# One attention kernel of two parts: three phases against eight interleaved chunks with a hand-kept order

## The chip, the cores and the metric

The kernel runs on one core of one Trainium2 chip. The metric is the device time of one execution in microseconds, from many executions of which the fast ones of a kernel agree within about 1.5%. "The profile" is one execution recorded by the hardware profiler; "the trace" is its list of instructions. The clock of TensorE is recorded as a share of its full speed. "Busy" is the recorded time of an engine's instructions.

## The reference

Two independent attentions over 2048 tokens with 32 heads of 20 columns (width 640); the outputs stand side by side.

```python
# A: four segments of 512 tokens; causal softmax inside a segment, plus a memory of earlier segments
for s in range(4):
    p = softmax(qs @ ks.T * scale + causal_mask);  a_dot = p @ vs
    pq = phi(qs);  a_mem = (pq @ M) / (pq @ z + 1e-6)      # phi(t) = t+1 if t>0 else exp(t)
    outs.append(g * a_mem + (1 - g) * a_dot)
    M = M + phi(ks).T @ vs;  z = z + phi(ks).sum()
A = concat(outs) @ wo
# B: causal attention in a sliding window of 256 tokens
B = (softmax(mask_window(q @ k.T * scale)) @ v) @ wo
```

## The kernel before

Heads are handled four at a time (a "group", eight groups), each head in its own 32 rows. The *scores* k·q of a head contract over 32 rows, so they use a 32-row tile of the array; the *values* p·v produce 32 output rows, so they use a 32-column tile. All projections, output projections and transposes use the whole array ("dense" below). The exponentials run on ScalarE, masks on GpSimd and VectorE, evacuations of PSUM on VectorE. (PSUM is the memory that TensorE writes to; an evacuation copies a result out of it.) The tile that a matmul uses, whole array, 32 rows, 32 columns or both, is called its tiling mode below, and a step from one to another a mode change.

The program has three phases: all projections of B and the k, v projections of A; then attention B, with the q projection of A interleaved as long as it lasts; then attention A with the output projections. This is B's inner loop:

```python
for kt in range(T):                                        # 16 key tiles of 128
    for hp in range(2):                                    # scores: two heads per PSUM tile
        for i in range(2):
            nc.tensor.matmul(pss[hp][:, i, 0:N], lhsT=kg[rows, ...], rhs=qg[rows, ...],
                             tile_position=(HD * q4, 0))   # a 32-row tile
    ...                                                    # exp on ScalarE, masks
    if kt % 2 == 1:
        for hp in range(2):
            for i in range(2):                             # values: head by head
                for n_, (_, k2, oc0, ncol, rc0) in enumerate(entries):
                    nc.tensor.matmul(O[orows, oc0:oc0 + ncol], lhsT=vg[:, k2, q4, 0:HD],
                                     rhs=pts[(hp, k2)][:, i, rc0:rc0 + ncol],
                                     tile_position=(0, HD * q4))   # a 32-column tile
        ...                                                # evacuate, transpose, normalise
    next(aux_gen, None)                                    # one piece of A's q projection
```

A's values (line 462) have the same order, hp, i, then key tile.

The softmax here doesn't subtract the row's maximum and nothing guards it: scores larger than these inputs give would overflow.

## Time and profile before

| | before |
|---|---|
| time, median of the first five runs | 808.9 us |
| TensorE / ScalarE / VectorE / GpSimd busy | 710 / 374 / 422 / 245 us |
| mean granted TensorE clock | 0.708 |

From the profile page of the kernel before: the first line's "busy us (share) xinstructions" of TensorE (PE), then the busy tenths of TensorE and ScalarE (ACT) in 40 slices of the span, and the granted clock in tenths.

```profile
...
PE 710.1 (88%) x4736; PEld 307.5 (38%) x4768; DVE 421.9 (52%) x1013; ACT 374.2 (46%) x498; POOL 244.9 (30%) x498
...
PE   2779969999999899999999888889988899889987
...
ACT  0000000046567876676665776246660666336650
...
PEclk9999989999999855555555555685558655585559
...
```

ScalarE does next to nothing (1.5 us) in the first fifth. The clock is near full in the first third and about half in most of the rest.

From the view by stretches of the kernel before; the columns are the stretch, its length, then busy us (and count) of TensorE, its weight loads, VectorE, ScalarE and GpSimd, and then the clock, the DMA share and GB/s.

```profile
...
120.00:160.00 40.00, 38.60 (x207) 18.76 (x210) 24.31 (x35) 0.00 (x0) 0.00 (x0) 1.00 0.58 183
240.00:280.00 40.00, 36.25 (x301) 17.15 (x300) 24.64 (x83) 30.91 (x46) 17.82 (x38) 0.98 0.55 165
278.00:430.00 152.00, 145.55 (x891) 55.57 (x889) 68.75 (x248) 104.76 (x143) 56.55 (x126) 0.50 0.11 31
...
```

For 152 us TensorE is busy 96% of the time and yet has half the clock. The q projection of A, the only projection in this phase, had run out at 252 us; of dense work only 70 transposes of 128 columns are left in the stretch, 13.8 us of TensorE. The Trainium skill ("TensorE: Matmul & The Clock Gate", Part 1) says that the clock is gated to half unless the array has been busy; that "busy" evidently isn't the busy time of the profile.

From the page, the chain that ended last, by engine. It is followed back from the last instruction, at each step to what ended that one's wait, its releaser:

```profile
...
PE 59%; DVE 10%; ACT 9%; POOL 8%; issue 6%; SPq 4%; DMA 2%; ACTq 0%; DVEq 0%; POOLq 0%
...
```

From the view of groups by form: line, engine, operation and shapes, count, then busy us and mean ns of one, and then idle time before and its releasers.

```profile
...
L305 ACT ACTIVATE pt<-psS 128x768 bf16<-128x768 f32 x224 | 171.7, 810 | 237.9 <-PE psS L298 197.8 <-issue 25.3 <-DVE oc L226 10.6
L437 ACT ACTIVATE pt<-ps 128x1024 bf16<-128x1024 f32 x128 | 126.9, 1023 | 85.2 <-PE ps L429 80.2 <-PE ps L462 4.5
...
```

### The profile page before, as it was taken

What the parts mean: (1) busy time and instruction counts of PE and PEld (TensorE: products, weight loads), DVE (VectorE), ACT (ScalarE), POOL (GpSimd) and SP (SyncE); (2) the same over time, 40 slices, a digit from 0 to 9 for tenths busy, and PEclk for the clock granted to TensorE, in tenths of its full rate; (3) what the DMA queues carried; (4) which work ended last, traced back from release to release, by engine and by line L of the source; (5) the groups of instructions that cost most, each with busy time, mean ns of one, the idle gap of its engine ahead of it and who ended that gap; (6) DMA issues with size and microseconds to landing.
All of it is one profiled execution on the core that took longest, in us unless ns stands there. A gap on an engine that the chain in (4) does not pass through costs nothing.

```text
span 807.3 us, 12210 instructions
## 1 busy us (share of the span) xinstructions
PE 710.1 (88%) x4736; PEld 307.5 (38%) x4768; DVE 421.9 (52%) x1013; ACT 374.2 (46%) x498; POOL 244.9 (30%) x498
## 2 busy tenths in 40 slices
PE   2779969999999899999999888889988899889987
PEld 1334524444444433333333333443335333443334
DVE  5356666566666544444444342555556455454435
ACT  0000000046567876676665776246660666336650
POOL 9000060024334433343333334113430333213430
PEclk9999989999999855555555555685558655585559
DMA  9923315641213604101000000420005000010001
GB/s 217 269 100 131 131 32 154 202 135 53 86 53 121 207 1 138 32 1 34 1 1 1 1 2 1 144 78 1 1 6 202 17 1 2 1 66 1 0 1 66
DMA packets 54028, 54.26 MB, mean 67 GB/s; under 512 B 22802, under 2 KB 46482, under 8 KB 53970
## 3 DMA queue, kind: packets, MB, share of 16 engines
q1 hardware_dynamic: 53970, 53.49, 21.6%
q8 instruction: 37, 0.61, 0.3%
q14 instruction: 21, 0.17, 0.1%
HBM read 24.38 MB, written 23.07 MB: 59 GB/s over the span
## 4 chain that ended last, share of the span: by engine, by line
PE 59%; DVE 10%; ACT 9%; POOL 8%; issue 6%; SPq 4%; DMA 2%; ACTq 0%; DVEq 0%; POOLq 0%
PE psO L341 11%; PE ps L462 10%; POOL pt L443 7%; PE psS L298 6%; ACT pt L437 6%; PE ps L262 5%; DVE oc L226 5%; PE pps L181 4%; PE ps L429 4%; PE pps L147 4%; PE pps L197 3%; PE ppa L181 3%; ACT pt L305 3%; SPq L528 2%; PE ps L228 2%
## 5 line engine op out<-in xcount | busy, mean ns | idle before, releaser
L305 ACT ACTIVATE pt<-psS 128x768 bf16<-128x768 f32 (+2 forms) x256 | 185.5, 770 | 247.3 <-PE psS L298 201.8
L437 ACT ACTIVATE pt<-ps 128x1024 bf16<-128x1024 f32 (+1 forms) x192 | 162.0, 882 | 97.3 <-PE ps L429 88.4
L443 POOL TENSOR_SCALAR_AFFINE_SELECT pt<-pt 128x256 bf16<-128x256 bf16 x256 | 107.0, 438 | 238.2 <-ACT pt L437 235.3
L313 POOL TENSOR_SCALAR_AFFINE_SELECT pt<-pt 128x256 bf16<-128x256 bf16 x224 | 104.2, 465 | 219.8 <-ACT pt L305 219.8
L462 PE MATMUL ps<-pt,v_s 128*32 128x128 bf16 (+3 forms) x512 | 117.9, 455 | 11.3 <-POOL pt L443 7.4
L341 PE MATMUL psO<-pt,vaug_B 128*32 128x256 bf16 (+1 forms) x960 | 125.5, 315 | 0.7 <-DVE pt L307 0.4
L307 DVE TENSOR_TENSOR pt<-pt,cmask 128x256 bf16<-128x256 bf16 x256 | 80.0, 313 | 52.0 <-ACT pt L305 50.5
L298 PE MATMUL psS<-qg,kg 32*128 32x384 bf16 (+2 forms) x512 | 100.2, 412 | 6.7 <-ACT pt L305 5.3
L429 PE MATMUL ps<-q_s,k_s 32*128 32x128 bf16 (+3 forms) x512 | 93.3, 433 | 7.5 <-ACT pt L437 6.0
L341 PEld LDWEIGHTS <-vaug_B 128*32 128x32 bf16 x960 | 59.8, 110 | 68.8 <-issue 57.2
L226 DVE CAST oc<-ps 128x512 bf16<-128x512 f32 x56 | 38.6, 689 | 79.4 <-PE ps L462 77.3
L462 PEld LDWEIGHTS <-v_s 128*32 128x32 bf16 x512 | 39.3, 119 | 75.4 <-issue 73.2
L226 DVE CAST oc<-psO 128x256 bf16<-128x256 f32 x64 | 27.1, 424 | 60.2 <-PE psO L341 60.1
L147 PE MATMUL pps<-xT_B,wallB 128*128 128x512 bf16 x196 | 47.4, 404 | 8.4 <-DMA wallB<-in_B_wqkv_dram 4.0
L228 PEld LDWEIGHTS <-oc 128*128 128x128 bf16 x352 | 27.7, 119 | 61.5 <-DVE oc L226 60.8
L298 PEld LDWEIGHTS <-kg 32*128 32x128 bf16 x512 | 25.1, 96 | 57.9 <-issue 50.1
L429 PEld LDWEIGHTS <-k_s 32*128 32x128 bf16 x512 | 20.4, 100 | 69.5 <-issue 67.6
L181 PE MATMUL ppa<-xT_A,wq_padA 128*128 128x512 bf16 x149 | 42.6, 380 | 4.3 <-DVE stp L184 2.4
L228 PE MATMUL ps<-ident,oc 128*128 128x128 bf16 x224 | 33.3, 302 | 14.5 <-DVE oc L226 14.5
L181 PE MATMUL pps<-xT_A,wk_padA 128*128 128x512 bf16 x156 | 36.6, 392 | 7.4 <-DVE wk_padA L133 6.9
L270 DVE CAST otile<-ps 128x640 bf16<-128x640 f32 x32 | 26.4, 825 | 23.0 <-PE ps L266 22.3
L147 PEld LDWEIGHTS <-wallB 128*128 128x128 bf16 x200 | 20.5, 103 | 34.6 <-issue 9.9
(95 smaller groups left out, 672.9 us busy)
## 6 DMA issues: line engine op xcount, KB each, us to landing
out_dram<-otile SPq DMA_DIRECT2D x32, 160.0 KB
vdA<-vstA SPq DMA_DIRECT2D x8, 512.0 KB
kdA<-stp SPq DMA_DIRECT2D x4, 1024.0 KB
qdA<-stp SPq DMA_DIRECT2D x4, 1024.0 KB
k_s<-kdA SPq DMA_DIRECT2D x4, 1024.0 KB
v_s<-vdA SPq DMA_DIRECT2D x4, 1024.0 KB
q_s<-qdA SPq DMA_DIRECT2D x4, 1024.0 KB
kcdB<-kcB SPq DMA_DIRECT2D x1, 2560.0 KB
```

The source lines that it names most:

```text
L147: nc.tensor.matmul(ps[:, 0:512], lhsT=w_ap[:, kt, m * P:(m + 1) * P], rhs=xT[:, kt, cs], start=(kt == 0), stop=(kt == KT - 1))
L181: nc.tensor.matmul(ps[:, 0:512], lhsT=wpad[:, kt, g * P:(g + 1) * P], rhs=xT[:, kt, cs], start=(kt == 0), stop=(kt == KT - 1))
L226: nc.vector.tensor_copy(out=oc[:, 0:ncols], in_=num_ps[:, 0:ncols])
L298: nc.tensor.matmul(pss[hp][:, i, 0:N], lhsT=kg[rows, kt * P:(kt + 1) * P], rhs=qg[rows, kt * P:kt * P + N], start=True, stop=True, tile_po ...
L305: nc.scalar.activation(out=pt[:, :, 0:N], in_=pss[hp][:, :, 0:N], func=ACT.Exp, scale=scale)
L307: nc.vector.tensor_tensor(out=pt[:, :, 0:P], in0=pt[:, :, 0:P], in1=self.cmask[:].unsqueeze(1).to_broadcast([P, 2, P]), op=ALU.mult)
L313: nc.gpsimd.affine_select(out=blk, in_=blk, pattern=[[0, 2], [-1, P]], compare_op=ALU.is_ge, fill=0.0, base=-1, channel_multiplier=1)
L341: nc.tensor.matmul(O[orows, oc0:oc0 + ncol], lhsT=vg[:, k2, q4, 0:HD], rhs=pts[(hp, k2)][:, i, rc0:rc0 + ncol], start=(n_ == 0), stop=(n_ ...
L429: nc.tensor.matmul(pss[hp][:, i, coloff[kt]:coloff[kt] + n], lhsT=k_s[rows, g, q0:q0 + P], rhs=q_s[rows, g, q0:q0 + n], start=True, stop=True,
L437: nc.scalar.activation(out=pt[:, :, 0:used], in_=pss[hp][:, :, 0:used], func=ACT.Exp, scale=scale)
L443: nc.gpsimd.affine_select(out=blk, in_=blk, pattern=[[0, 2], [1, P]], compare_op=ALU.is_ge, fill=0.0, base=0, channel_multiplier=-1)
L462: nc.tensor.matmul(NUM[orows, P * kt:P * kt + n], lhsT=v_s[:, kt, h, 0:HD], rhs=pt[:, i, co:co + n], start=(cnt == 1), stop=(cnt == nmm), ...
```

## The change

The intent: keep TensorE and ScalarE busy at the same time from start to end. The kernel is nearly rewritten; this is its core.

```diff
-  phase 1: all projections; phase 2: attention B (+ A's q projection); phase 3: attention A
+  chunks = [("A", 0), ("B", 0), ("A", 1), ("B", 1), ("A", 2), ("B", 2), ("A", 3), ("B", 3)]
+  # every chunk: 512 queries, 8 groups x 3 score banks x 2 head pairs = 48 "slots" (384 in all)
+  with self.tc.manual_schedule():            # instructions stay in the order they are written
+      for t, (n, kind, c, banks, g, b, pair) in enumerate(slots):
+          if t == start[n]: seed(n + 1)      # projections of the next chunk become filler
+          fl.force(t)                        # filler whose deadline is now
+          pt = self.scores(banks, b, pair, g, k, q, koff)      # + one exp of up to 1024 columns
+          self.masks(...)
+          # finished group: values 3 slots later, transposes 5, normalisation 6 slots later
+          fl.run(t, extra, kind == "A" and c > 0 and t % 2 == 1)   # filler, as credit allows
 ...
+  def av(...):                               # values: key tile by key tile, over the four heads
+      for n_, (_, kt, q0, nq, b, c0) in enumerate(ent):
+          for j in range(4):
+              nc.tensor.matmul(O[HD * j:HD * j + HD, ...], ..., tile_position=(0, HD * j))
 ...
+  def final_job(self, o_tok, b, wo, out_rows):    # output projection as filler, 32 jobs
+      transposes; yield 5 * mm_ns(128)
+      nc.vector.tensor_copy(out=oT[:], in_=t[:, 0:self.KT * P])
+      yield 600.0
+      for hf in range(2): 5 matmuls of 320 columns each; copy to ot
+      nc.sync.dma_start(out=out_rows, in_=ot[:])
 ...
-  A's q and k projected with padded weights: 8 blocks of 128 rows for each 512 columns
+  projected compactly (5 blocks), stored to DRAM, and spread to 32 rows a head by DMA
```

`fl` is a queue of generators. It gives each slot as much filler as spreads what is left evenly, and with the last argument true it gives none.

## The prediction

> **What bounds the kernel now (808.9 us).** Three phases. The view by stretches shows projections in 0-160 us, with ScalarE busy only 1.5 us; then sliding-window attention B until about 510 us; then segments A. TensorE bounds it: 710 us busy (88%), 59% of the chain that ended last; ScalarE 374, VectorE 422, GpSimd 245. Two things make TensorE slow. (1) The granted clock is about 1.00 until 278 us, then 0.50 except in bursts at the output projections (mean 0.71). From 280 to 440 us TensorE is busy 38.3 of every 40 us and still gets 0.50; what had ended was the dense 128-row q projection of A, interleaved until 252 us. The Trainium skill ("TensorE: Matmul & The Clock Gate", Part 1) says activity releases the throttle; here narrow 32-row/32-column work alone did not suffice. (2) In the timeline, the attention-times-values matmuls (lines 341, 462) run head by head: in A the next tile of a head starts about 390, 310, 100 ns after the last at half clock, so four heads take about 3.4 us.
>
> **What the change does.**
> - Eight chunks (A, B alternating), with projections, output projections and memory updates as filler between score tiles: the serial 160 us goes, and dense work (half of TensorE's time) spreads over the span, so I expect a clock near 1.0.
> - Attention times values goes key tile by key tile over four heads: tiled neighbours start 3 to 13 ns apart in the trace, so 512+384+256+128 columns should take about 0.53 us at full clock.
> - Exps of B are 192 of up to 1024 columns, not 256 of 768; A's q/k projections lose their padding (8 blocks to 5), except in chunk 0.
> - Added: spreading of heads through DRAM by strided DMAs, and many alternations of tiling mode. A change of mode costs 95-100 ns at full clock in the trace (dense to score 310 against 215; score to value 260 against 160). The Trainium skill ("TensorEngine Tiling (Array Packing)", Key Properties) calls it a drain; the trace agrees.
>
> **Sums (estimates from durations in the trace).** TensorE at full clock: scores 73, values 37, memory and updates 10, q/k projections 93, v 43, output 52, transposes 24, so about 330; plus about 700 mode changes in the built order at 95 ns, 67: about 396 us. ScalarE: 0.94 us for 1024 columns back to back, 0.73 for 768: 325 plus 33 phi exps 20, about 345. VectorE about 335 (fewer masks and casts), GpSimd 285. So TensorE still bounds, ScalarE close behind. Start: the first projection began at 27 us; now one 512-row chunk and one weight suffice, about 11 us. 11 + 396 + 5 cold start + 4 at the end = 416 if TensorE never waits. For waits on exps, evacuations and chunk boundaries I add 5 to 12%: **448 us, range 415 to 500**. Faster by over 2%: 0.97; within 2%: 0.02; slower: 0.01. Practically all of the gain lies on the critical path, as TensorE is the path.
>
> **What would show it.** Mean clock above 0.9; TensorE over 90% busy, ScalarE 75-85%; first exp before 20 us; the four value matmuls of one key tile about 13 ns apart; mode changes of about 95 ns; VectorE about 335 us.
>
> **What would make it wrong.** The clock falls to 0.5 in chunks with little filler (the last B chunk, or odd slots in A, where filler is held). Column-tiled matmuls interleaved over heads may not overlap. VectorE evacuations with four shared PSUM buffers, VectorE and GpSimd slowing each other, or DMA spreading at chunk boundaries could stall the in-order TensorE queue above 12%. If TensorE and ScalarE overlap better: about 420.

## More of the kernel before

An output projection transposes a token tile on TensorE, copies it with VectorE and multiplies it at once. The order of instructions on each engine is the framework's scheduler's; it may move them as the dependencies allow.

From the timeline of TensorE in the kernel before, in a later segment of A: start, duration until the last of the merged matmuls ended, line, tile names, count.

```profile
...
564.14 0.61 PE L462 MATMUL ps<-pt,v_s 128*32 128x512 bf16 x1
564.68 0.39 PE L429 MATMUL ps<-q_s,k_s 32*128 32x256 bf16 x2
565.01 0.88 PE L462 MATMUL ps<-pt,v_s 128*32 128x384 bf16 x2
565.82 0.61 PE L429 MATMUL ps<-q_s,k_s 32*128 32x256 bf16 x4
566.75 1.25 PE L462 MATMUL ps<-pt,v_s 128*32 128x256 bf16 x8 [0.32 <-POOL pt L443]
567.94 0.60 PE L429 MATMUL ps<-q_s,k_s 32*128 32x512 bf16 x1
568.48 1.25 PE L462 MATMUL ps<-pt,v_s 128*32 128x256 bf16 x5
569.66 0.60 PE L429 MATMUL ps<-q_s,k_s 32*128 32x512 bf16 x2
...
```

Line 462 is the values of one group, 16 matmuls, and line 429 is scores of the next group. The scheduler has cut the 16 value matmuls into pieces of 1, 2, 8 and 5, with scores between. From the first value matmul to the last piece's end is 5.6 us, at a clock of 0.50.

## The result, and the profile after

The changed kernel takes 485.9 us (median of nine; one of them, 496.5, counts as slow), the kernel before 809.7 us beside it. The ratio is 0.600 (0.5987 to 0.6011); here and below a ratio is the mean time of a kernel's fast runs over that of the other's of the same rounds, so it is not quite the ratio of the medians. The time lies within the predicted range, 38 us above the central value.

| | before | after | predicted |
|---|---|---|---|
| span in the profile | 807.3 | 484.2 | |
| TensorE busy | 710 | 421 (87%) | over 90% |
| ScalarE busy | 374 | 356 (74%) | 345 (75 to 85%) |
| VectorE / GpSimd busy | 422 / 245 | 323 / 263 | 335 / 285 |
| mean clock | 0.708 | 0.974 | over 0.9 |
| first exp of a score | 169.0 | 15.7 | before 20 |

The page of the changed kernel, same lines:

```profile
...
PE 421.3 (87%) x4770; PEld 195.6 (40%) x4806; DVE 322.8 (67%) x690; ACT 356.3 (74%) x419; POOL 263.4 (54%) x551
...
PE   2999998898978998979896999898988799899965
...
ACT  1346678879677777878986777697888677799930
...
PEclk9999999899799999999999999999989999999979
...
```

ScalarE works from the first slices on, beside TensorE, and the clock is full but for a few short dips and the end.

Its chain that ended last, by engine:

```profile
...
PE 61%; DVE 16%; ACT 13%; issue 5%; DMA 3%; POOL 1%; SPq 1%; POOLq 0%; ACTq 0%; DVEq 0%
...
```

TensorE has as large a share of the path as before. Its groups of exponentials:

```profile
...
L335 ACT ACTIVATE pt<-sc 128x1024 bf16<-128x1024 f32 x288 | 285.5, 1029 | 77.1 <-PE sc L328 67.3 <-POOL pt L341 3.9 <-POOL pt L347 1.1
...
L335 ACT ACTIVATE pt<-sc 128x512 bf16<-128x512 f32 x80 | 47.7, 597 | 26.9 <-PE sc L328 26.4 <-POOL pt L347 0.2
...
```

A piece is as long as before (1023 and 600 ns). The prediction counted 0.94 us for 1024 columns, from exps that follow each other without a pause; in the changed kernel such exps start 0.92 us apart. The timeline of TensorE in an A chunk:

```profile
...
262.45 0.44 PE L439 MATMUL m<-ident,o_tok 128*128 128x128 bf16 x5
264.60 0.72 PE L449 MATMUL m<-wo_A,oT 128*128 128x320 bf16 x4 [1.71 <-DVE oT L443]
265.25 0.40 PE L328 MATMUL sc<-qA,kA 32*128 32x512 bf16 x6
265.58 0.73 PE L390 MATMUL m<-pt,vA 128*32 128x512 bf16 x16
266.24 0.39 PE L402 MATMUL m<-pqA,MZ 32*32 32x512 bf16 x4
266.57 0.72 PE L449 MATMUL m<-wo_A,oT 128*128 128x320 bf16 x4
...
```

All 16 value matmuls of a group (line 390) are together, and the next thing starts 0.66 us after the first, against 5.5 us from 564.14 to 569.66 in the fence of before, where the clock was half. The second line shows what the prediction missed in size: between the transposes of an output projection (line 439) and its matmuls (line 449) TensorE stood idle for 1.71 us, waiting for VectorE to copy the transposed tile. From the view of waits, TensorE's matmuls alone: who waited for whom, us in all, times, longest.

```profile
...
PE m L449 <- DVE oT L443: 21.1, 22, 1.7
PE m L178 <- DMA wk_A<-in_A_wk_dram: 9.7, 1, 9.7
PE m L414 <- DVE oc L408: 7.0, 8, 1.5
PE sc L328 <- ACT pt L335: 5.6, 20, 0.4
...
```

How much does TensorE wait in all? I compared each interval between the starts of neighbouring matmuls with what they need without waiting: the columns over the clock, and 95 ns where the tiling mode changes. The first matmul starts at 9.7 us and the last ends at 480.3, so 470.6 us; the excess over need is 70.7 us, which leaves 400 us of need. The prediction's sum was 396. Of the excess, 24.5 us stand before line 449 with the copy as releaser, 13.0 before scores with an exp as releaser, and 7.8 before transposes of values with their evacuation as releaser. (This is more than in the view of waits, since a matmul's recorded end lies after the start of the next: a dense one of 512 columns is recorded with some 380 ns, and the next starts 216 ns after it.)

Two cautions. The trace lacks the records of 36 dense matmuls of 512 columns (line 195; 4770 matmuls of 4806). At 0.216 us each they look like up to 8 us of waiting, so the waits are nearer 63 us and the need nearer 408. And the level depends on the small allowances of such a count: a second count gave 75 to 81 us here and 42 to 47 us in e8 below, where I had 70.7 and 36.9; the difference between the two runs, 34 us, is the same.

The same reading of the traces counts changes of tiling mode: 928 in the kernel before, 703 in the changed one (708 as built). The change did not add them; the old schedule was full of them. The price of 95 ns holds in the changed kernel too: from a dense matmul of 512 columns to a score it takes 312 ns, to another dense one 216.

### The profile page after: what moved, and what is told of

The parts are those of the page before. It is cut to its first block, busy times and chain, and to the rows that moved or that the text cites. A ratio compares the mean times of both kernels' runs of the same rounds, so it can differ in the third digit from the quotient of the medians.

```text
span 484.2 us, 11853 instructions
## 1 busy us (share of the span) xinstructions
PE 421.3 (87%) x4770; PEld 195.6 (40%) x4806; DVE 322.8 (67%) x690; ACT 356.3 (74%) x419; POOL 263.4 (54%) x551
## 4 chain that ended last, share of the span: by engine, by line
PE 61%; DVE 16%; ACT 13%; issue 5%; DMA 3%; POOL 1%; SPq 1%; POOLq 0%; ACTq 0%; DVEq 0%
PE sc L328 14%; ACT pt L335 12%; PE m L195 12%; PE m L449 8%; PE m L297 7%; PE m L390 7%; PE m L414 5%; PE m L178 4%; DVE st L199 2%; DVE oc L408 2%; DVE oT L443 2%; DMA scr_kB<-st 1%; ACT e L231 1%; DVE o_tok L428 1%; DVE pqc L233 1%
## 5 line engine op out<-in xcount | busy, mean ns | idle before, releaser
L335 ACT ACTIVATE pt<-sc 128x1024 bf16<-128x1024 f32 (+2 forms) x384 | 340.5, 930 | 105.9 <-PE sc L328 95.3
L341 POOL TENSOR_SCALAR_AFFINE_SELECT pt<-pt 128x256 bf16<-128x256 bf16 (+1 forms) x336 | 168.2, 504 | 177.2 <-ACT pt L335 175.5
L347 POOL TENSOR_SCALAR_AFFINE_SELECT pt<-pt 128x256 bf16<-128x256 bf16 x176 | 81.2, 463 | 24.1 <-ACT pt L335 21.1
L408 DVE CAST oc<-m 128x512 bf16<-128x512 f32 x88 | 58.4, 687 | 40.8 <-PE m L390 40.2
L328 PE MATMUL sc<-qB,kB 32*128 32x128 bf16 (+2 forms) x704 | 73.9, 280 | 5.3 <-ACT pt L335 3.1
L199 DVE CAST st<-m 128x512 bf16<-128x512 f32 x70 | 47.2, 685 | 24.5 <-PE m L195 15.5
L328 PE MATMUL sc<-qA,kA 32*128 32x128 bf16 (+3 forms) x512 | 52.9, 304 | 5.0 <-ACT pt L335 2.5
L195 PE MATMUL m<-xT,wB 128*128 128x512 bf16 x185 | 48.9, 381 | 1.3 <-DVE st L199 0.4
L297 PE MATMUL m<-wv_A,xT 128*128 128x320 bf16 x160 | 33.4, 339 | 1.2 <-DVE o_tok L428 1.2
L428 DVE TENSOR_TENSOR o_tok<-m,rr 128x320 bf16<-128x320 bf16 x64 | 31.5, 491 | 2.2
```

The source lines that it names most:

```text
L195: nc.tensor.matmul(ps[:, :], lhsT=w_ap[:, kt, m * P:(m + 1) * P], rhs=xT[:, kt, :], start=(kt == 0), stop=(kt == self.KT - 1))
L199: nc.vector.tensor_copy(out=st[:, m, :], in_=ps[:, :])
L297: nc.tensor.matmul(ps[:, 0:320], lhsT=xT[:, kt, tt * P:(tt + 1) * P], rhs=w_ap[:, kt, 320 * hf:320 * hf + 320], start=(kt == 0), stop=(kt ...
L328: nc.tensor.matmul(ps[:, i, c0:c0 + nq * P], lhsT=k[rows, g, kc:kc + P], rhs=q[rows, g, q0 * P:(q0 + nq) * P], start=True, stop=True, tile ...
L335: nc.scalar.activation(out=pt[:, :, lo:hi], in_=ps[:, :, lo:hi], func=ACT.Exp, scale=self.scale)
L341: self.nc.gpsimd.affine_select(out=blk, in_=blk, pattern=[[0, 2 * n], [1, P]], compare_op=ALU.is_ge, fill=self.zero, base=0, channel_multi ...
```

## The experiments

The theory after the result: TensorE bounds the changed kernel, its need is as summed, the clock is held up by dense filler, and the missing 38 us are waits, above all for the copy of an output projection. The rival for the bound: ScalarE and latencies set the pace, and TensorE has slack. All kernels gave correct results. All profiles are of fast runs; a median is that of all runs of a kernel, of which e5 and its control had one slow one each.

### e1: transposing ahead

```diff
-for b in range(LT): fl.add(..., self.final_job(o_tok, b, ...))      # T(b), copy, multiply(b)
+fl.add(..., self.final_jobs(o_tok, ...))    # T(0); then for each b: T(b+1), multiply(b)
```

> The changed kernel, but the four output projections of a chunk are one job that transposes block b+1 before it multiplies block b, so that VectorE's copy of the transposed block is hidden. Same work, 709 instead of 708 mode changes. Theory (TensorE bounds the changed kernel, and its waits on that copy, about 24 us of some 71 us of waits in the trace, lie on its path): 15 to 25 us less, about 465 us; the waits of the output matmuls (line 449 of the changed kernel) on the copy nearly gone. Rival (the pace is set by ScalarE and the chain of latencies around it, TensorE has slack): under 5 us, the waits come back elsewhere, as waits of scores on exps.

Measured: 473.8 us, ratio to before 0.5846, so 12 us less than the changed kernel. TensorE's waits in e1:

```profile
...
PE m L414 <- DVE oc L408: 12.0, 11, 1.9
...
PE sc L328 <- ACT pt L335: 5.5, 20, 0.5
PE m L459 <- DVE oT L446: 3.7, 3, 1.4
...
```

The waits for the copy (now line 459) fell from 21.1 us to 3.7, but those for the evacuation of values (line 414) rose from 7.0 to 12.0. That is the theory's direction, with a gain somewhat below the 15 to 25 us it expected. Besides the new waits, the mean clock of the profiled run is 0.962 instead of 0.974, which is 5 us of full clock lost in addition.

### e8 and e9: later transposes of values; filler after every slot

```diff
 # e8 = e1 and:
-at(t + 2, 224.0 * nm, s2)      # transposes of a finished value group
-at(t + 3, 0.0, s3)             # normalisation
+at(t + 4, 224.0 * nm, s2)
+at(t + 5, 0.0, s3)
 # e9 = e8 and:
-fl.run(t, extra, kind == "A" and c > 0 and t % 2 == 1)
+fl.run(t, extra, False)
```

> e1 with the transposes of a finished value group two score tiles later (and its normalisation too), so that VectorE's evacuation is through before TensorE gets there. 707 mode changes. Theory: most of the 13 us in which e1's TensorE waits for that evacuation (line 408) go, about 463 us. Rival (these waits are replaced by others, as half of e1's were): over 470 us.

> e8 with filler allowed after every score tile in A too: 825 mode changes instead of 707. Theory: 118 x 95 ns = 11 us more on TensorE, against up to 10 us less waiting for exps: within 8 us of e8. Rival (mode changes count for nothing, smaller lumps only help ScalarE): at least 8 us faster than e8.

e8 took 460.7 us, ratio 0.5679 (0.5658 to 0.5699), better than both kernels: 0.5679 / 0.5999 = 0.947 of the changed one. Its page and its waits:

```profile
...
PE 421.5 (92%) x4806; PEld 196.2 (43%) x4806; DVE 321.1 (70%) x690; ACT 353.1 (77%) x419; POOL 262.4 (57%) x551
...
```

```profile
...
PE sc L328 <- ACT pt L335: 7.3, 25, 0.5
PE m L248 <- DVE pk L233: 5.0, 5, 1.5
...
PE m L459 <- DVE oc L408: 0.8, 2, 0.4
PE m L414 <- DVE oc L408: 0.8, 1, 0.8
...
```

TensorE is 92% busy; the waits of output matmuls and of value transposes are 0.8 us each, and only 0.3 us of waiting for the copy is left in the full list. By the comparison of starts the excess fell from 70.7 to 36.9 us, and the time by 25. Of these 34 us some 8 are the records that the trace of the changed kernel lacks (e8's lacks none), so about 26 stand against 25. So these waits lay on the path. e9 took 468.1 us, 7.4 more than e8: the 118 extra mode changes were not free, as the theory had it.

### e2: filler in larger lumps

```diff
-fl.run(t, extra, kind == "A" and c > 0 and t % 2 == 1)
+fl.run(t, extra, t % 2 == 1)
```

> The changed kernel, with filler only after every other score tile in all chunks (it did so only in A chunks after the first): 511 instead of 708 mode changes in the built order, same matmuls. Theory (each change costs about 95 ns of TensorE's time and TensorE bounds): 197 x 95 ns = 19 us less, about 467 us, if larger lumps of filler starve ScalarE no more than now. Rival (TensorE has slack, or lumps starve ScalarE): no gain or a loss, with more idle time of ScalarE before exps.

Measured: 486.7 us, no gain. TensorE's busy time fell by 16 us (421 to 405), but by the comparison of starts its waits rose from 71 to 96 us, of which those of scores for exps rose from 13 to 29. Larger lumps pay back in waiting what they save in mode changes. For the price of a mode change this run alone settles nothing.

### e5 and its control: the price of a mode change

```diff
 # in scores(), before the real matmuls, which overwrite the result
+nc.tensor.matmul(ps[:, 0, 0:16], lhsT=self.ident[:], rhs=self.ident[:, 0:16], ...)        # e5: dense
+nc.tensor.matmul(ps[:, 0, 0:16], lhsT=k[j0:j0+HD, ...], ..., tile_position=(j0, 0))        # control
```

> The changed kernel, with one full-array matmul of 16 columns before each score tile, whose result the scores overwrite: 384 matmuls and 208 more mode changes (916). Theory: 208 x 95 ns = 20 us more than the control with the same 384 matmuls in the tiling of the scores, about 505 to 515 us in all. Rival (TensorE has slack for it): under 5 us more than the control.

> Control: the same 384 added matmuls of 16 columns, but in the scores' own 32-row tiling, so no mode change is added (708). Theory and rival: 384 x 10 to 25 ns, so 4 to 10 us more than the changed kernel if TensorE bounds, nothing if it has slack.

e5 took 524.4 us, the control 495.2, each with one slow run; the fast runs alone have medians of 521.7 and 494.7. That is 27 us, or 26 by the ratios (0.6447 and 0.6126, each with an interval of some 3 us either way), for 208 mode changes; e5 as a whole lies above the expected 505 to 515. The control itself cost 9 us for 384 matmuls of 16 columns, 24 ns each. TensorE has no slack for either, which the rival needed. The difference is more than 208 x 95 ns = 20 us. The mean clock of the profiled e5 is 0.950 (of 517.9 us) against 0.969 (of 489.9 us), so it lost 25.9 - 15.2 = 11 us of full clock more; the two together, 31 us, are of the size of the difference. That the clock fell because of the changes is argued, not shown.

### b2: is it dense work that holds the clock?

```diff
 # the kernel before, in attention B, once A's q projection has run out
+ps = dummy_ps()
+for kq in range(2):
+    nc.tensor.matmul(ps, lhsT=dummy_w[:, kq, 0:P], rhs=dummy_x[:, kq, 0:512], ...)
```

> The kernel before, with two full-array matmuls of 512 columns added to each key tile of B once the real interleaved projection is used up (their result is never read). Theory (dense work lets TensorE keep the full clock, narrow work alone does not): the clock stays near 1.0 until B ends instead of falling to 0.50 at 278 us, and although work is added the time falls by about 20 us, to about 790. Rival (the clock falls for another reason, such as the time or the load): 0.50 as before, and about 90 x 1 us more, about 900 us.

Measured: 802.1 us, ratio 0.9899 (0.988 to 0.9918). The stretch of the table above, with the added work:

```profile
...
278.00:430.00 152.00, 151.39 (x1149) 63.83 (x1147) 78.61 (x278) 114.88 (x160) 69.54 (x141) 1.00 0.09 24
...
```

The clock stayed at 1.00 through B (until 429.7 us; before, until 278), and ScalarE did 115 us of work in this stretch instead of 105. A kernel that does more work is 1% faster; its interval leaves out 1. So added dense work raises the clock here. It also raised TensorE's busy share from 96% to 99.6%, and no run added narrow matmuls instead; but the share alone is not the cause, since the changed kernel has 0.974 with TensorE 87% busy. The gain, 8 us, is smaller than the 20 us expected, probably because the added matmuls (some 184, at 0.22 us each about 40 us) and 143 more mode changes use up most of what the clock gives; that was not tested apart.

### e6: the changed kernel without interleaving

```diff
-fl.run(t, extra, kind == "A" and c > 0 and t % 2 == 1)
+fl.run(t, extra, True)                       # filler only when its deadline forces it
-fl.add(10 ** 6, ..., self.final_job(...))
+fl.add(t + 51, ..., self.final_job(...))     # a deadline for the output projections
```

> The changed kernel, with no filler between score tiles: projections run only when a chunk needs them, output projections a chunk later, each in a burst. Same matmuls, 375 instead of 708 mode changes. Theory (interleaving is what keeps both engines busy and the clock up): ScalarE idles through the bursts and the clock falls between them, 550 to 650 us, mean clock under 0.85. Rival (the gain is from less work; interleaving adds only mode changes): about 485 us less 32, so 450 to 490.

Measured: 654.3 us, ratio 0.807, mean clock 0.781. TensorE, ScalarE and the clock in 40 slices:

```profile
...
PE   3777888778778997778877898778886798877775
...
ACT  1445265862638542983736735398173946358810
...
PEclk9967888569885889658779597955969868975569
...
```

The clock and its fall are as expected, the time is 4 us above the range. ScalarE drops to 1 to 3 tenths in the bursts, and the clock falls between them, to 5 or 6 tenths. It gives a split of the 324 us: 810 - 654 = 156 us come with chunks, grouping and less work, even in bursts; 654 - 486 = 168 us come from interleaving, the higher clock included.

### b1, e4, e4b: does the order of heads matter?

```diff
 # b1: the kernel before (both attentions); e4 is the reverse, in the changed kernel
-for hp in range(2):
-    for i in range(2):
-        for n_, ... in enumerate(entries): matmul(...)
+for n_, ... in enumerate(entries):
+    for hp in range(2):
+        for i in range(2): matmul(...)
 # e4b: head by head, in two passes
+for part in (ent[:4], ent[4:]):
+    for j in range(4):
+        for ... in part: matmul(...)
```

> The kernel before, with one part of the change alone: the attention-times-values matmuls go key tile by key tile over the four heads, in both attentions, instead of head by head. Same matmuls. Theory (tiles of different heads overlap when they stand next to each other): at half clock a group of A falls from about 3.4 to about 1.1 us (32 groups, 74 us), and B gets near the pace of its exps where the clock is 0.50 (about 45 us), so about 690 us. Rival (head by head they already overlap enough, or exps and masks set the pace): less than 40 us, above 770.

> The changed kernel, with its attention-times-values matmuls put back head by head (same matmuls and mode changes). Theory (their overlap over heads is part of the gain): about 1.2 us more for each group of A and 1.3 to 1.8 for each of B, 64 groups, so 60 to 90 us more if TensorE bounds, about 545 to 575 us. Rival (not on the path): under 15 us.

> The changed kernel, value matmuls head by head again, but in two passes: the first four key tiles of each head, then the last two. In e4 the groups of A (four matmuls a head) overlapped fully even head by head, those of B (six a head) did not: 1.79 us a group instead of 0.77. Theory (each column group takes up to four matmuls ahead, in order): B groups back at 0.75 to 0.9 us, all within 5 us of the changed kernel. Rival (the look-ahead is a number of matmuls over all heads, and the last of a head's first four block it): B groups above 1.2 us, 10 us or more slower.

b1 took 757.9 us (0.936): 52 us less, where the theory expected 120. e4 took 505.0 us: 19 us more, where it expected 60 to 90. Both miss by far, so the theory of head order falls as I had put it. The trace of e4 shows why. The built order of one A group there is 512, 384, 256, 128 columns of head 0, then the same of heads 1 to 3. The starts in the trace (ns after the first, and columns; only one matmul of a head has 512 columns in A):

```
e4, A group:  0:512 13:512 27:512 40:512   227:384 242:384 254:384 268:384   389:256 ...   498:128 ...
e4, B group:  0:384 173:384 335:256 341:384 444:256 515:384 553:128 ... 1636:128   (six a head)
e4b, B group: 0:384 14:384 27:384 40:384   174:384 187:384 201:384 215:384   336:256 ...
```

TensorE itself started head 1's first matmul 13 ns after head 0's, ahead of three matmuls that stand before it in the program. The Trainium skill ("TensorE: Matmul & The Clock Gate", Part 3, "What overlaps and what doesn't") says that matmuls start in program order, without reordering; here they do not, for tiles in different columns. With six matmuls a head, head 1 started only at 341 ns, when head 0's third had begun, that is when at most four of head 0 were unfinished. This fits a queue of four for each column tile. e4b tests it: with passes of at most four, a B group takes 0.80 us, as against 1.79 in e4 and 0.77 in the changed kernel. Its time, 492.5 us (0.6067), is about 6 us above the changed kernel's, just outside the 5 us that its theory allowed; the clock of its profile is 0.962 instead of 0.974, about 6 us of full clock, but whether that is the reason is not tested. So in the changed kernel the order of heads is worth about 19 us, nearly all in B, where e4 spends 24 groups x 1.02 us = 24 us more on TensorE; a group of A takes 0.69 us instead of 0.66.

In the kernel before, order and cutting up work together. By the intervals between starts, its value matmuls took 232 us of TensorE and 168 in b1, its scores 209 and 223: 50 us less, about what b1 gained. In the built order of A before, the pieces of 1, 2, 8 and 5 matmuls lie in 1, 1, 3 and 2 column tiles, so the short ones have no neighbour in another tile to overlap with; in b1 nearly all pieces are of 2 or 4 matmuls, each in another column tile. That is the likely reason why head order is worth 52 us there and next to nothing in A of e4, where the 16 stand together. b1 did not remove the cutting up: it raised the mode changes from 928 to 1093 in the trace. What the cutting alone costs in that kernel no run shows.

### e7: the same program without the kept order

```diff
-with self.tc.manual_schedule():
-    self.body(...)
+self.body(...)
```

> The changed kernel without its hand-kept order: the framework's scheduler is let loose on the same program, as it is in the kernel before. 739 mode changes instead of 708 in the built order. Theory (keeping value matmuls together and filler between scores is what the kept order is for): 30 us or more slower, with value groups cut up by score matmuls. Rival (the writing order alone does it): within 10 us of 486.

Measured: 525.4 us, 39 more than with the kept order, 739 mode changes instead of 703 to 708, mean clock 0.912. TensorE's waits in it:

```profile
...
PE sc L328 <- ACT pt L335: 16.4, 35, 1.2
PE m L390 <- POOL pt L347: 12.1, 11, 3.1
PE m L449 <- DVE oT L443: 10.8, 18, 0.9
...
```

The scheduler put value matmuls where their masked tiles were not ready (12.1 us instead of 1.7) and let scores wait for exps (16.4 instead of 5.6). But the waits for the copy (line 449) fell from 21.1 us to 10.8, so these waits together grew by some 11 us only. The larger part seems to go with the clock: 1 - 0.912 of 524.8 us is 46 us of full clock lost, instead of 13 in the changed kernel. Why the clock is lower in this order was not tested. So keeping the order is worth 39 us here. That the same scheduler cut up the groups of the kernel before is likely, but no run kept that kernel's order by hand.

## Why the prediction was right or wrong

- **Bound by TensorE: right.** It has 59% and 61% of the path before and after, and small additions to it (e5, its control) and removals of its waits (e1, e8) moved the time. It was 87% busy and not over 90%, for the waits below.
- **TensorE's need, 396 us: right.** The trace gives 400, or some 408 with the missing records.
- **The clock: right, and shown.** 0.974 with filler, 0.781 in bursts (e6), and 1.00 instead of 0.50 by added dense work (b2).
- **Start and engines: near.** First exp at 15.7 us. ScalarE 356 instead of 345, VectorE and GpSimd somewhat lower than summed.
- **The term that was mis-sized: "for waits on exps, evacuations and chunk boundaries I add 5 to 12%", 20 to 48 us.** They measured 70.7 us (some 63 if the missing records are taken out), and that puts 448 at about 486. With the waits as allowed the time would have stayed under about 465; it lies within the range because the range, to 500, was wider than its own sum. The largest part is one that the prediction named only in general, as an evacuation: 24.5 us of output matmuls waiting for VectorE's copy of the tile that TensorE had just transposed. Thirty-two such round trips stand inside the filler, and in the trace the scores behind one wait too (the idle 1.71 us above). e1 and e8 took these and the evacuation waits away, and the time fell by 25 us.
- **Why the values were slow: half wrong.** "Head by head" is not enough as the reason for 3.4 us a group: where a group stands together, head order costs only 0.03 us in A (e4). In the cut-up order of the kernel before it was worth 52 us (b1), of the 120 that I put on it. For the changed kernel's sum the reason did not matter, and that was luck. The size predicted for the changed kernel, 0.53 us, was near: 0.55 at best, 0.66 with the mode change that follows.
- **"Added: many alternations of tiling mode": wrong sign.** The price, 95 to 100 ns, was right in the trace, and the Trainium skill ("TensorEngine Tiling (Array Packing)", Key Properties) is confirmed in kind; but there were 928 before and 703 after. I had counted the changed kernel and not the old one.
- **"B until about 510 us": misread.** Its last exp starts at 440.7 us; the clock's rise at 520 us belongs to output projections. Nothing in the sum rested on it.

## What to carry to other kernels

When one engine does nearly everything, count three things in the built order and not only its work: the changes of tiling mode, the dense share in each stretch (the clock was 0.50 without dense projections and 1.00 with dense work in b2), and every place where it needs something back from another engine. Issue such a round trip one or two steps ahead, so that other work stands between the two halves; here that was worth 5% (e8). When a kernel is narrow-tiled for a long stretch, spread its dense work over it instead of doing it first (0.974 against 0.781 in bursts, e6).

## What the Trainium skill lacked or had wrong

- "TensorE: Matmul & The Clock Gate", Part 3, says that matmuls are never reordered. In e4, matmuls of the next heads started 13, 27 and 40 ns after the first, ahead of earlier ones of the heads before; the look-ahead fits four for each column tile (e4 against e4b: 1.79 and 0.80 us a group).
- The same page, Part 1, speaks of how busy the array is. A stretch that is 96% busy, all but 13.8 of 145.5 us with 32-row and 32-column tiles, had a clock of 0.50, and two dense matmuls of 512 columns for each key tile raised it to 1.00 (b2). It does not say that narrow tiles count for less.
- "TensorEngine Tiling (Array Packing)", Key Properties, names the drain at a mode change but no price: 95 to 100 ns at full clock in these traces, and 26 to 27 us for 208 changes in e5 over its control, part of which may be the clock.
